# Three attention units transposed by DMA instead of TensorE, and a hand-written order of 1,080 steps laid out anew

## The chip, the cores and the metric

The kernel runs on one core of a Trainium2 chip. The metric is the device time of one execution in microseconds (us). Before the change it is 202.87 us, the median of three runs (202.74 to 204.03).

A core has five instruction queues, each of which takes its instructions strictly in order: TensorE (PE in the profile, with its weight loads as PEld), VectorE (DVE), ScalarE (ACT), GpSimd (POOL) and SyncE (SP). PE writes to PSUM, the matmul memory; the other operands lie in SBUF. Loads and stores are DMAs, issued here from SP, from POOL and at two places from ACT.

## The reference

Attention with a decay, in blocks of 64 positions, and behind it a two-layer network with a leaky rectifier. Cut to what is computed:

```python
# q, k, v: [4, 8, 768, 64]; lam: one decay for each of 8 heads
for b in range(768 // 64):
    qb, kb, vb = q[:, :, sl], k[:, :, sl], v[:, :, sl]
    intra = einsum(einsum(qb, kb) * Dmask, vb)      # within the block, masked by lam**(i-j)
    inter = einsum(qb * lam_pow, kv_state)          # from the blocks before
    out[:, :, sl] = intra + inter
    kv_state = lam_block * kv_state + einsum(kb * rev_pow, vb)
x = out.transpose(0, 2, 1, 3).reshape(3072, 512)
h = x @ w_in                                        # 512 x 2048
g = maximum(h, 0) + alpha * minimum(h, 0)
result = g @ w_out                                  # 2048 x 512, float32
```

## The kernel before

**Tiling.** The 3,072 rows are cut into six chunks `c` of 512 (two batches of 256 positions each). The attention of a chunk is four units `n` = 4c to 4c+3: two batches `bi` times two halves `hh` of the heads. Units 0 to 3 feed chunk 0, units 4 to 7 chunk 1, and so on. The network runs for a chunk when its four units are done.

**One unit.** `load` brings q and k as float32 in halves of 256 KB (quarters of a chunk's 1 MB) or whole, from SP, or from POOL where its last argument is "G". `load_v16` (line 268) brings v through POOL, cast to fp16 on the way. `cast(n, "q16", E)` and `cast(n, "k16", E)` (257) make fp16 copies `qk` on engine E: "A" is ACT, "V" DVE, "G" POOL. The copies are transposed into `qkT`, in one of two ways: `turn` (309) does four (or eight) 128 by 128 transposes on PE into a PSUM bank, and `turn_copy` (323) brings them to SBUF on E; `turned` (299) does all of it as one DMA transpose from SP. Then come `score_products` (PE), `masked` (DVE, times the decay mask), `inter` and `intra` (PE, into the accumulator), `attended` (the accumulator to SBUF on ACT or DVE), and for the running state `key_decayed`, `state_products`, `states` or `state_in` and `first_state`. `decayed` scales the transposed q. There is one PSUM buffer `s` for the scores, so `score_products` of a unit waits until `masked` of the unit before has read it. Units 0 to 8 are transposed on PE, units 9 to 23 by DMA.

**The network.** `up(c, f)` is one 512 by 128 column of h (four matmuls of 512 rows), `relu` (ACT) and `prelu` (DVE) make g from it. Chunk 0 multiplies g by `w_out` in the plain way, with `down(0, t, part)`, four matmuls each; `part` p needs block p of `w_out`, which `load_wout(p)` brings. The later chunks use sums of blocks in place of some of the products: `w_sum` forms sums of `w_out`, `in_sum` of `w_in`, `g_sum` of g and `x_sum` of x, each a run of elementwise operations on DVE or, with "G", on POOL; `second` and `last` are the products of the second layer, and `first` those of the first layer for chunks 4 and 5. `first_x`, `first_d`, `second_x` and `second_out` put the results together.

**What sets the order.** The schedule is manual. Every engine's queue holds its instructions in the order of the calls from line 799 to the end. Three things besides data hold an engine up: a free PSUM bank (four of them rotate among transposes, h, y and state products), `gate` (111), a two-byte DMA on SP that reads a piece of `w_out` and so holds SP's later loads until that block has landed, and the pair `vector_turn(i)` / `gpsimd_waits(i)` (560, 563): the first remembers the newest DVE instruction, the second makes the newest POOL instruction wait for it. There are 21 such waits before the change.

Of the kernel before, what the change touches and what calls it, by code (L numbers as in the profile page):

```python
# [11 lines left out]
def kernel(  # L12
# [503 lines left out]
    def prelu_half(c, f, bi):  # L516
        prelu_of(c, f, bi, "V")
# [341 lines left out]
    key_decayed(3)  # L859
    turn(2, (1,))  # L860
    first_state(1)
    inter(1)
    turn(3, (0,))
    turn_copy(2, (1,), "A")
    turn_copy(2, (0,), "V")
    masked(0)
    intra(1)
    score_products(2)
    decayed(2)
    turn_copy(3, (0,), "V")  # L870
    state_in(2, 0)
    first_state(0)
    masked(2)
    decayed(3)
    attended(1, "A")
    first_state(2)
    state_in(2, 1)
    turn(3, (1,))
    load(1, 0, "q", 0, "G")
    inter(0)  # L880
    load(1, 0, "k", 0, "G")
    load_v16(4)
    intra(0)
    load_win(2)
    states(2, (1,))
    slopes_turn()
    load(1, 0, "q", 1, "G")
    state_in(3, 0)
    turn_copy(3, (1,), "A")
    score_products(3)  # L890
    attended(0, "A")
    load(1, 0, "k", 1, "G")
    query_decay(2, 0)
    slopes()
    inter(2)
    intra(2)
    first_state(3)
    load(1, 1, "q", 0, "G")
    masked(3)
    state_in(1, 1)  # L900
    state_in(3, 1)
    attended(2, "A")
    states(3, (1,))
    state_in(0, 1)
    inter(3)
    states(1, (1,))
    intra(3)
    up(0, 4, 0)
    attended(3, "A")
    load(1, 1, "k", 1, "G")  # L910
    up(0, 5)
    states(0, (1,))
    relu(0, 5)
    cast(4, "q16", "G")
    up(0, 7)
    prelu(0, 5)
    up(0, 6)
    relu(0, 4, 0)
    prelu_half(0, 4, 0)
    load_wout(0)  # L920
    up(0, 3)
    key_decayed(4)
    relu(0, 7)
    up(0, 15)
    relu(0, 6)
    load_v16(5)
    prelu(0, 7)
    up(0, 13)
    relu(0, 3)
    prelu(0, 6)  # L930
    load(1, 1, "q", 1, "G")
    up(0, 14)
    relu(0, 15)
    prelu(0, 3)
    relu(0, 13)
    prelu(0, 15)
    prelu(0, 13)
    up(0, 4, 1)
    up(0, 0)
    up(0, 1)  # L940
    relu(0, 14)
    state_products(4, None, True)
    relu(0, 4, 1)
    prelu_half(0, 4, 1)
    relu(0, 0)
    prelu(0, 14)
    load_wout(1)
    relu(0, 1)
    turn(4, (0,))
    prelu(0, 0)  # L950
    prelu(0, 1)
    cast(5, "q16", "G")
    up(0, 10)
    up(0, 2)
    first_state(4)
    turn_copy(4, (0,), "V")
    turn(5, (0,))
    states(4, (1,))
    relu(0, 10)
    relu(0, 2)  # L960
    cast(4, "k16", "G")
    up(0, 11)
    cast(5, "k16", "A")
    relu(0, 11)
    decayed(4)
    prelu(0, 10)
    turn_copy(5, (0,), "V")
    up(0, 8)
    in_sum(1, 1, "G")
    turn(4, (1,))  # L970
    prelu(0, 2)
    load_wout(2)
    relu(0, 8)
    inter(4)
    cast(6, "q16", "A")
    prelu(0, 11)
    up(0, 9)
    turn_copy(4, (1,), "V")
    relu(0, 9)
    turn(5, (1,))  # L980
    load_wout(3)
    turn_copy(5, (1,), "V")
    up(0, 12)
    relu(0, 12)
    score_products(4)
    down(0, 3, 0)
    prelu(0, 9)
    prelu(0, 8)
    decayed(5)
    prelu(0, 12)  # L990
    key_decayed(5, "A")
    turn(6, (0,))
    down(0, 0, 0)
    masked(4)
    down(0, 2, 0)
    score_products(5)
    w_sum(1, 1)
    gate(2, "out")
    intra(4)
    in_sum(1, 3)  # L1000
    in_sum(1, 0, "G")
    state_products(5)
    first_state(5)
    load(1, 1, "k", 0)
    cast(7, "q16", "G")
    turn_copy(6, (0,), "V")
    w_sum(1, 2)
    key_decayed(7)
    down(0, 0, 1)
    states(5, (1,))  # L1010
    query_decay(0, 0)
    load_v16(7)
    down(0, 3, 1)
    down(0, 2, 1)
    turn(7, (0,))
    masked(5)
    down(0, 3, 2)
    attended(4, "V")
    cast(7, "k16", "G")
    turn_copy(7, (0,), "V")  # L1020
    down(0, 2, 2)
    turn(7, (1,))
    down(0, 0, 2)
    turn_copy(7, (1,), "A")
    inter(5)
    w_sum(2, 2)
    down(0, 2, 3)
    decayed(6)
    score_products(7)
    cast(6, "k16", "V")  # L1030
    intra(5)
    load(2, 0, "k", 0)
    load(2, 0, "q", None)
    query_decay(1, 0)
    state_products(7)
    first_state(7)
    down(0, 1, 0)
    w_sum(1, 3, "G")
    down(0, 3, 3)
    attended(5, "A")  # L1040
    key_decayed(6, "V")
    vector_turn(1)
    query_decay(3, 0)
    masked(7)
    w_sum(2, 3)
    down_copy(0, 2)
    decayed(7)
    w_sum(2, 1, "G")
    load_v16(6)
    down(0, 0, 3)  # L1050
    turn(6, (1,))
    states(7, (1,))
    load_v16(8)
    down_copy(0, 3)
    load(2, 1, "k", None)
    w_sum(1, 0)
    inter(7)
    load(2, 0, "k", 1)
    key_decayed(8)
    gpsimd_waits(1)  # L1060
    w_sum(2, 0, "G")
    w_sum(3, 1)
    down(0, 1, 1)
    cast(8, "k16", "A")
    load_v16(9)
    up(1, 3, 0)
    turn_copy(6, (1,), "V")
    score_products(6)
    down_copy(0, 0)
    cast(9, "q16", "A")  # L1070
    cast(8, "q16", "A")
    intra(7)
    w_sum(4, 3)
    vector_turn(2)
    state_in(6, 0)
    w_sum(3, 0, "G")
    gpsimd_waits(2)
    relu(1, 3, 0)
    turn(8, (0, 1))
    attended(7, "A")  # L1080
    first_state(6)
    down(0, 1, 2)
    masked(6)
    inter(6)
    intra(6)
    turn_copy(8, (0, 1), "V")
    prelu_half(1, 3, 0)
    state_products(8)
    score_products(8)
    w_sum(4, 1, "G")  # L1090
    gpsimd_waits(2)
    state_in(6, 1)
    key_decayed(10, "A")
    attended(6, "V")
    down(0, 1, 3)
    cast(9, "k16", "A")
    states(8, (0, 1))
    up(1, 15)
    up(1, 14)
    load(2, 1, "q", 0)  # L1100
    states(6, (1,))
    relu(1, 15)
    down_store(0, 3)
    load(3, 0, "q", None)
    down_copy(0, 1)
    load(2, 1, "q", 1)
    cast(10, "k16", "A")
    up(1, 7)
    prelu(1, 15)
    key_decayed(9)  # L1110
    relu(1, 7)
    turned(9)
    masked(8)
    up(1, 11)
    decayed(8)
    load_v16(14)
    cast(10, "q16", "G")
    relu(1, 14)
    load(3, 1, "k", 1)
    relu(1, 11)  # L1120
    prelu(1, 7)
    up(1, 6)
    relu(1, 6)
    cast(11, "k16", "A")
    inter(8)
    prelu(1, 14)
    w_sum(3, 2, "G")
    prelu(1, 11)
    up(1, 0)
    prelu(1, 6)  # L1130
    up(1, 8)
    relu(1, 0)
    prelu(1, 0)
    up(1, 13)
    score_products(9)
    relu(1, 8)
    load(3, 1, "k", 0)
    relu(1, 13)
    intra(8)
    load_v16(12)  # L1140
    prelu(1, 8)
    state_products(9)
    cast(12, "q16", "A")
    cast(11, "q16", "G")
    up(1, 12)
    up(1, 5)
    relu(1, 12)
    load_v16(10)
    masked(9)
    prelu(1, 13)  # L1150
    decayed(9)
    prelu(1, 12)
    up(1, 3, 1)
    relu(1, 5)
    attended(8, "A")
    up(1, 2)
    cast(13, "q16", "A")
    turned(10)
    g_sum(1, 1, 1, 1, "G")
    up(1, 1)  # L1160
    key_decayed(11)
    prelu(1, 5)
    load(3, 0, "k", None)
    relu(1, 3, 1)
    load_v16(13)
    relu(1, 2)
    g_sum(1, 3, 1, 1, "G")
    up(1, 4)
    states(9, (0, 1))
    w_sum(3, 3, "G")  # L1170
    relu(1, 1)
    in_sum(1, 2, "G")
    inter(9)
    prelu_half(1, 3, 1)
    prelu(1, 2)
    prelu(1, 1)
    up(1, 9)
    up(1, 10)
    relu(1, 4)
    relu(1, 9)  # L1180
    turned(11)
    down_store(0, 2)
    relu(1, 10)
    intra(9)
    prelu(1, 4)
    score_products(10)
    prelu(1, 9)
    prelu(1, 10)
    cast(13, "k16", "A")
    state_products(10)  # L1190
# [718 lines left out]
```

## Time and profile before

| | before |
|---|---|
| median of three runs | 202.87 us |
| the profiled execution, whole | 202.76 us |
| its span, first to last instruction | 201.0 us |
| granted TensorE clock, mean | 0.998 |
| DMA packets | 30.53 MB, 152 GB/s over the span |

The profile is of one execution. The 1.8 us between its time and its span lie around the program. Busy time of PE is the time in which a matmul is under way; matmuls are pipelined, so the cost of one in a run is the distance from its start to the next one's, which is shorter than its own duration. In the timeline, rows of like instructions are merged: "x8" with a start and a length, and in brackets the idle time before them and what ended it.

### The profile page before, as it was taken

How to read it: one execution, taken by the hardware profiler on the slowest of the kernel's cores; microseconds unless marked ns; L12 is line 12 of the kernel's file. 1: busy time of each engine (PE TensorE's matmuls, PEld its weight loads, DVE VectorE, ACT ScalarE, POOL GpSimd, SP SyncE). 2: the span in 40 equal slices, each digit the busy share in tenths (PEclk: the TensorE clock that was granted, in tenths of full speed). 3: DMA queues.
4: the chain of work that ended last, by engine and by line, in shares of the span. 5: the costliest groups of instructions: out<-in, count | busy, mean ns of one | idle time of the engine just before them, and what ended most of it. 6: DMA issues, size and time to landing. Idle time of an engine off the chain costs nothing. (4 is left out here: it accounts for less than half of the span.)

```text
span 201.0 us, 5883 instructions
## 1 busy us (share of the span) xinstructions
PE 193.1 (96%) x2351; PEld 129.3 (64%) x2351; DVE 169.9 (85%) x309; ACT 133.3 (66%) x296; POOL 154.1 (77%) x171
## 2 busy tenths in 40 slices
PE   7889999999999999999999999998999999999892
PEld 7766445556545688665556758775656566888792
DVE  6787998958899997999999998899999999993610
ACT  4886768229788799885688784347587886742021
POOL 8999999777999469999999989942877027559900
PEclk9999999999999999999999999999999999999999
DMA  5999999999999999999999971010310101031053
GB/s 155 265 226 225 251 255 230 200 239 281 229 193 228 298 209 214 194 185 205 201 197 220 141 164 69 3 55 0 106 52 5 54 0 52 3 104 52 19 180 117
DMA packets 59199, 30.53 MB, mean 152 GB/s; under 512 B 29652, under 2 KB 57956, under 8 KB 59172
## 3 DMA queue, kind: packets, MB, share of 16 engines
q1 hardware_dynamic: 41236, 19.87, 41.6%
q0 software_dynamic: 17776, 10.23, 33.2%
q8 instruction: 18, 0.29, 0.6%
q14 instruction: 9, 0.07, 0.1%
q10 hardware_dynamic: 160, 0.07, 0.1%
HBM read 27.27 MB, written 6.29 MB: 167 GB/s over the span
## 5 line engine op out<-in xcount | busy, mean ns | idle before, releaser
L498 PE MATMUL h_ps<-xT,w_in_sb 128*128 128x512 f16 (+1 forms) x264 | 59.4, 373 | 0.0
L655 PEld LDWEIGHTS <-g 128*128 128x128 f16 x464 | 44.6, 98 | 8.9
L526 DVE SCALAR_TENSOR_TENSOR g<-m,oma,h_ps 128x512 f16<-128x512 f32 (+1 forms) x66 | 46.0, 725 | 3.7 <-ACT m L511 2.2
L511 ACT ACTIVATE m<-h_ps 128x512 f32<-128x512 f32 (+1 forms) x66 | 36.7, 584 | 14.5 <-PE h_ps L498 13.7
L498 PEld LDWEIGHTS <-w_in_sb 128*128 128x128 f16 x264 | 24.7, 98 | 24.8
L388 DVE TENSOR_TENSOR sm<-s,dmask 128x1024 f16<-128x1024 f32 x24 | 29.2, 1217 | 2.0 <-PE s L377 1.8
L655 PE MATMUL y<-w_out_sb,g 128*128 128x256 f16 x224 | 27.1, 273 | 0.0
L341 POOL TENSOR_TENSOR qdT<-qkT,qdecay 128x512 f16<-128x512 f16 (+1 forms) x23 | 23.7, 1038 | 2.8 <-DVE qkT L249 2.0
L655 PE MATMUL b<-t,g 128*128 128x256 f16 x160 | 19.9, 273 | 0.0
L272 POOL DMA_DIRECT2D v<-in_v_dram x24 | 18.9, 789 | 0.0
L290 ACT ACTIVATE kdec<-kraw,kdecay 128x64 f16<-128x64 f32 x72 | 18.0, 341 | 0.0
L247 ACT ACTIVATE xT<-acc 128x512 f16<-128x512 f32 x21 | 12.5, 596 | 8.0 <-PE acc L422 5.4
L457 DVE SCALAR_TENSOR_TENSOR R<-R,rdecay,acc 128x128 f16<-128x128 f16 x54 | 15.5, 339 | 0.8 <-ACT xT L247 0.6
L576 POOL TENSOR_TENSOR s<-g,g 128x512 f16<-128x512 f16 x10 | 11.4, 1151 | 5.9 <-DVE g L526 5.9
L573 POOL TENSOR_TENSOR g<-g,g 128x512 f16<-128x512 f16 x12 | 14.1, 1198 | 2.3 <-DVE g L526 1.3
L534 PE MATMUL o_ps<-w_out_sb,g 128*128 128x512 f16 x64 | 15.4, 380 | 0.0
L247 ACT ACTIVATE o_sb<-y 128x512 f32<-128x512 f32 (+2 forms) x12 | 6.3, 524 | 10.5 <-PE y L697 5.4
L573 POOL TENSOR_TENSOR g<-s,g 128x512 f16<-128x512 f16 x5 | 5.9, 1174 | 9.5 <-DVE g L573 9.5
L292 POOL TENSOR_TENSOR kdec<-kraw,kdecay 128x512 f16<-128x512 f32 x12 | 12.7, 1061 | 0.5 <-DMA kraw<-in_k_dram 0.5
L573 POOL TENSOR_TENSOR g<-g 128x512 f16<-128x512 f16 x10 | 11.4, 1154 | 1.1 <-DVE g L526 0.7
L576 POOL TENSOR_TENSOR w_in_sb<-g,g 128x512 f16<-128x512 f16 x3 | 3.9, 1285 | 9.0 <-DVE g L526 9.0
L377 PE MATMUL s<-qkT 64*64 64x128 f16 x384 | 9.8, 220 | 0.9 <-DVE sm L388 0.9
(131 smaller groups left out, 381.7 us busy)
## 6 DMA issues: line engine op xcount, KB each, us to landing
out_dram<-o_sb SPq DMA_DIRECT2D x23, 256.0 KB, 2.4
kraw<-in_k_dram SPq DMA_DIRECT2D x7, 512.0 KB, 6.0
qraw<-in_q_dram SPq DMA_DIRECT2D x6, 512.0 KB, 5.6
v<-in_v_dram POOLq DMA_DIRECT2D x24, 128.0 KB, 6.0
w_in_sb<-in_moe_w_in_dram POOLq DMA_DIRECT2D x4, 512.0 KB, 8.6
w_out_sb<-in_moe_w_out_dram POOLq DMA_DIRECT2D x4, 512.0 KB, 9.4
qraw<-in_q_dram POOLq DMA_DIRECT2D x6, 256.0 KB, 7.3
qraw<-in_q_dram SPq DMA_DIRECT2D x6, 256.0 KB, 6.6
```

The source lines that it names most:

```text
L247: nc.scalar.activation(out, in_, AF.Copy)
L272: nc.gpsimd.dma_start(out=v16.rearrange("p h e d -> p h (e d)"), in_=v[2 * (c % 2) + bi, ds(4 * hh, 4), ds((c // 2) * W, W), :].rearrange( ...
L290: nc.scalar.activation(kdec[:, e, h], kr[:, e, h], AF.Copy, scale=kdecay[:, x, e : e + 1])
L341: engine(eng).tensor_tensor(out=qdT[:, :, :, p], in0=(t["qps"] if eng == "P" else t["qkT"][:, 0])[:, :, :, p], in1=qdecay[:, hh, :, :, p], ...
L388: nc.vector.tensor_tensor(out=t["sm"].rearrange("p a h x j -> p (a h) x j"), in0=t["s"].rearrange("p a h x j -> p (a h) x j"), in1=mask_of ...
L457: nc.vector.scalar_tensor_tensor(out=R[b, hh, m + 1][:, hp], in0=R[b, hh, m][:, hp], scalar=rdecay[:, 2 * hh + hp : 2 * hh + hp + 1], in1= ...
L498: nc.tensor.matmul(h[:, 0:n] if bi is None else h[:, 0:n].rearrange("p (e j) -> p e j", e=2), lhsT=w_in_sb[:, gi, ts(f, 128)], rhs=x.rearr ...
L511: nc.scalar.activation(m[:, 0:n], HP[c, f, bi][:, 0:n], AF.Relu, scale=-1.0)
L526: engine(eng).scalar_tensor_tensor(out=g, in0=m, scalar=oma[:, f : f + 1], in1=h, op0=ALU.mult, op1=ALU.add)
L534: nc.tensor.matmul(O[c, t], lhsT=g_of(c, f)[:, t // 2, t % 2, :], rhs=w_out_sb[:, f, :], start=(f == 0), stop=(f == NF - 1),)
L573: engine(eng).tensor_tensor(out=out, in0=a, in1=b, op=ALU.subtract)
L655: nc.tensor.matmul(Y[c, k][:, ds(b * HALF, HALF)], lhsT=left(c, i, f, b), rhs=right(i, f), start=(f == 0 and b == 0 and i in (1, 5)), stop ...
```

## The change

The first 60 calls of the order stay. Behind them:

- Units 6, 7 and 8 are transposed with `turned` (SP) in place of `turn` and `turn_copy`: 24 transposes on PE and five copies (four on DVE, one on ACT) go, three DMA transposes come.
- All calls behind the first 60 are in a new order. Among others, unit 7 comes before unit 6, `load_win(2)` and two halves of unit 7's data are issued before the data of units 4 and 5, `load_wout(0)` to `load_wout(3)` come earlier in the order, and more of the `down` products of chunk 0 stand ahead of `score_products(5)`.
- 79 calls change engine, with the same arithmetic: casts, `turn_copy`, `w_sum`, `g_sum`, `in_sum`, `x_sum`, `attended`, `decayed`. Of the last chunks (4 and 5), ten `g_sum` go from POOL to DVE and five the other way.
- The waits of POOL for DVE are 29 in place of 21.

The lines that matter most here, from the diff (it has 1,819 lines):

```diff
@@ -857,1022 +857,1028 @@
     decay_mask(0)
     score_products(0)
     key_decayed(3)
+    first_state(1)
     turn(2, (1,))
-    first_state(1)
+    state_in(1, 1)
+    first_state(0)
+    masked(0)
     inter(1)
+    intra(1)
     turn(3, (0,))
+    load_win(2)
+    turn_copy(2, (0,), "V")
     turn_copy(2, (1,), "A")
...
+    load(1, 1, "q", 1, "G")
+    turn(3, (1,))
+    decayed(2, "V")
+    attended(1, "A")
     score_products(2)
...
-    load(1, 0, "q", 0, "G")
-    inter(0)
-    load(1, 0, "k", 0, "G")
-    load_v16(4)
     intra(0)
-    load_win(2)
...
-    load(1, 0, "q", 1, "G")
...
+    state_in(3, 1)
+    load(1, 0, "k", 0, "G")
+    inter(2)
+    masked(3)
+    load(1, 1, "k", 1, "G")
+    first_state(3)
+    load(1, 0, "q", 0, "G")
...
+    load_v16(4)
...
+    state_in(2, 1)
     load(1, 0, "k", 1, "G")
-    query_decay(2, 0)
+    load(1, 0, "q", 1, "G")
     slopes()
...
     up(0, 4, 0)
+    load_wout(0)
     attended(3, "A")
-    load(1, 1, "k", 1, "G")
+    load_wout(1)
+    relu(0, 4, 0)
+    in_sum(1, 2, "G")
+    up(0, 4, 1)
+    states(3, (1,))
+    up(0, 6)
+    up(0, 3)
...
     key_decayed(4)
+    up(0, 0)
+    relu(0, 14)
+    load(1, 1, "q", 0, "G")
     relu(0, 7)
-    up(0, 15)
...
+    cast(5, "q16", "G")
+    cast(7, "q16", "V")
     prelu(0, 7)
     up(0, 13)
...
+    load_wout(2)
+    relu(0, 2)
+    cast(7, "k16", "G")
+    cast(4, "q16", "A")
+    state_products(4, None, True)
+    prelu(0, 10)
     relu(0, 13)
-    prelu(0, 15)
+    key_decayed(7)
+    load_wout(3)
+    gate(2, "out")
+    prelu(0, 2)
+    w_sum(1, 0, "G")
+    up(0, 8)
+    turn(5, (0,))
+    load(1, 1, "k", 0)
+    first_state(4)
+    prelu(0, 0)
+    load(2, 0, "k", 0)
     prelu(0, 13)
-    up(0, 4, 1)
-    up(0, 0)
-    up(0, 1)
-    relu(0, 14)
-    state_products(4, None, True)
...
+    cast(4, "k16", "V")
+    vector_turn(1)
+    prelu(0, 9)
     turn(4, (0,))
-    prelu(0, 0)
-    prelu(0, 1)
-    cast(5, "q16", "G")
-    up(0, 10)
-    up(0, 2)
-    first_state(4)
+    in_sum(1, 0, "G")
+    gpsimd_waits(1)
     turn_copy(4, (0,), "V")
-    turn(5, (0,))
+    relu(0, 11)
+    load_v16(5)
+    down(0, 3, 0)
+    prelu(0, 11)
+    turn(4, (1,))
+    decayed(4)
+    down(0, 2, 0)
+    up(0, 12)
+    load_v16(6)
+    relu(0, 12)
+    turn_copy(4, (1,), "A")
+    down(0, 3, 1)
+    query_decay(2, 0)
+    down(0, 2, 1)
     states(4, (1,))
-    relu(0, 10)
-    relu(0, 2)
-    cast(4, "k16", "G")
...
+    in_sum(1, 3)
+    vector_turn(2)
+    prelu(0, 12)
+    score_products(4)
+    turn(5, (1,))
+    down(0, 0, 0)
+    cast(6, "q16", "G")
     inter(4)
-    cast(6, "q16", "A")
-    prelu(0, 11)
...
     decayed(5)
-    prelu(0, 12)
     key_decayed(5, "A")
-    turn(6, (0,))
-    down(0, 0, 0)
+    w_sum(1, 1, "G")
+    gpsimd_waits(2)
+    down(0, 2, 2)
+    w_sum(2, 1, "G")
+    gpsimd_waits(2)
+    down(0, 3, 2)
+    turn_copy(5, (1,), "A")
+    w_sum(4, 1)
     masked(4)
-    down(0, 2, 0)
+    down(0, 3, 3)
+    turned(7)
+    w_sum(1, 2)
+    down(0, 2, 3)
     score_products(5)
-    w_sum(1, 1)
-    gate(2, "out")
+    w_sum(2, 0)
+    vector_turn(3)
+    load_v16(7)
+    down_copy(0, 3)
...
     intra(4)
-    in_sum(1, 3)
-    in_sum(1, 0, "G")
     state_products(5)
+    cast(6, "k16", "A")
     first_state(5)
...
-    cast(7, "q16", "G")
-    turn_copy(6, (0,), "V")
-    w_sum(1, 2)
-    key_decayed(7)
...
+    cast(8, "k16", "G")
+    load_v16(8)
+    query_decay(1, 0)
+    load(2, 0, "q", None)
...
+    key_decayed(6, "V")
+    w_sum(1, 3)
+    vector_turn(4)
     states(5, (1,))
     query_decay(0, 0)
-    load_v16(7)
-    down(0, 3, 1)
-    down(0, 2, 1)
-    turn(7, (0,))
     masked(5)
-    down(0, 3, 2)
-    attended(4, "V")
-    cast(7, "k16", "G")
-    turn_copy(7, (0,), "V")
-    down(0, 2, 2)
-    turn(7, (1,))
+    down(0, 1, 0)
+    down(0, 1, 1)
+    load_v16(9)
+    decayed(7, "V")
+    vector_turn(5)
+    down(0, 1, 2)
+    turned(6)
...
-    turn(8, (0, 1))
...
+    turned(8)
...
+    g_sum(5, 2, 1, 1)
+    vector_turn(18)
     second(4, 5, 1)
-    second_store(3, 7)
-    prelu(5, 15)
-    g_sum(4, 2, 0, 1)
-    g_sum(5, 1, 1, 1, "G")
-    second(5, 2, 0)
-    second(5, 2, 1)
+    second(5, 5, 1)
+    g_sum(5, 2, 0, 1, "G")
...
```

## What I predicted

> **What bounds the kernel now.** I read the page first: busy time, then the slices.
>
> ```profile
> span 201.0 us, 5883 instructions
> ...
> PE 193.1 (96%) x2351; PEld 129.3 (64%) x2351; DVE 169.9 (85%) x309; ACT 133.3 (66%) x296; POOL 154.1 (77%) x171
> ...
> PE   7889999999999999999999999998999999999892
> ...
> DVE  6787998958899997999999998899999999993610
> ...
> PEclk9999999999999999999999999999999999999999
> DMA  5999999999999999999999971010310101031053
> ```
>
> PE is busy for nine tenths or more of nearly every slice from the fourth on, at full clock: the kernel is PE's stream with a start and a tail. The DMA row matters too: its engines are full to slice 23, about 115 us. How little PE waits stands in the view of waits, PE alone; only these two lie behind the start:
>
> ```profile
> PE b L780 <- DVE e L576: 0.6, 1, 0.6
> PE y L697 <- POOL g L573: 0.6, 1, 0.6
> ```
>
> So a saving counts only if it shortens PE's stream or one of these waits, and any new wait of PE is paid in full. I add up against this execution, 202.76 us with its 1.8 us around the span; that is 0.11 under the median of 202.87.
>
> **Term 1, the transposes.** Five groups go, for units 6, 7 and 8: 24 transposes. PE's timeline has the cost of a group as the distance to the next row:
>
> ```profile
> 27.18 1.89 PE L498 MATMUL h_ps<-xT,w_in_sb 128*128 128x512 f16 x8
> 28.90 0.39 PE L316 MATMUL tp<-ident,qk 128*128 128x128 f16 x4
> ...
> 34.45 0.39 PE L316 MATMUL tp<-ident,qk 128*128 128x128 f16 x4
> 34.68 1.89 PE L534 MATMUL o_ps<-w_out_sb,g 128*128 128x512 f16 x8
> ...
> 36.75 0.39 PE L402 MATMUL acc<-sm,v 64*64 64x128 f16 x16
> 36.97 0.29 PE L422 MATMUL acc<-v,kdec 64*64 64x64 f16 x16
> ...
> 49.68 0.62 PE L316 MATMUL tp<-ident,qk 128*128 128x128 f16 x8
> 50.13 1.03 PE L534 MATMUL o_ps<-w_out_sb,g 128*128 128x512 f16 x4
> ```
>
> Four cost 34.68 - 34.45 = 0.23, eight 0.45: in all four fours and the eight, 4 x 0.23 + 0.45 = 1.37 us off the stream. The first two rows give the price of an `up` or a `down`: 1.72 / 8 x 4 = 0.86; the rows at 36.75 and 36.97 that of one group of attention products, 0.22. The mean length of one transpose, from the groups by form, is no price, as lengths overlap:
>
> ```profile
> L316 PE MATMUL tp<-ident,qk 128*128 128x128 f16 x72 | 6.5, 220 | 0.6 <-DVE qk L249 0.6
> ```
>
> [...]
>
> The copies that go (four on DVE, one on ACT) are hidden: PE waited for neither engine there. The three DMA transposes come on SP:
>
> ```profile
> qkT<-qk SPq DMA_TRANSPOSE x15, 4.7
> ...
> DMA to landing us min/median/max: 3.0/4.7/8.3
> ```
>
> `turned(7)` has its casts early and stands behind the gate on `w_out` block 2 and two loads (about 40 us); PE comes to `score_products(7)` at about 48 (below), so it is hidden even at 8.3. `turned(6)` and `turned(8)` have 7 to 9 us; price zero, and up to 2 us at the longest time. Behind them on SP stand only loads for chunk 2.
>
> **Term 2, a wait that comes in.** POOL's queue decides here. `cast(5, "q16", "G")` needs the half `load(1, 0, "q", 1)`. Before, two halves, one v and a block of `w_in` were issued ahead of it (behind the third `w_in` block); now it is the last of eight: `load_win(2)`, six halves, one v. Eight of the same sizes followed that block before, too, in another order; here are the block and the eighth (timeline, then the DMA issues of two short windows):
>
> ```profile
> 10.81 0.83 POOL L98 DMA_DIRECT2D w_in_sb<-in_moe_w_in_dram  x1
> ...
> 21.72 0.75 POOL L89 DMA_DIRECT2D kraw<-in_k_dram  x1 [0.36 <-DMA w_in_sb<-in_moe_w_in_dram]
> ```
>
> ```profile
> w_in_sb<-in_moe_w_in_dram POOLq DMA_DIRECT2D x1, 512.0 KB, 10.6
> ...
> kraw<-in_k_dram POOLq DMA_DIRECT2D x1, 256.0 KB, 8.3
> ```
>
> The block landed at 10.8 + 10.6 = 21.4, the eighth at 21.7 + 8.3 = 30.0, so eight such transfers take 8.6 us with the DMA engines full. The prefix is the same, the eight are the same sizes: I expect `load(1, 0, "q", 1)` at 30.0, however early it is issued. Before, the cast ran here:
>
> ```profile
> 27.43 0.61 POOL L251 CAST qk<-qraw 128x512 f16<-128x512 f32 x1 [0.18 <-DMA qraw<-in_q_dram]
> 27.99 0.61 POOL L251 CAST qk<-kraw 128x512 f16<-128x512 f32 x1
> 28.60 0.67 POOL L341 TENSOR_TENSOR qdT<-qkT,qdecay 128x256 f16<-128x256 f16 x1
> 29.23 1.15 POOL L576 TENSOR_TENSOR s<-w_in_sb 128x512 f16<-128x512 f16 x1
> 30.33 1.53 POOL L104 DMA_DIRECT2D w_out_sb<-in_moe_w_out_dram  x2
> ...
> 34.49 1.04 POOL L292 TENSOR_TENSOR kdec<-kraw,kdecay 128x512 f16<-128x512 f32 x1
> 35.48 0.79 POOL L272 DMA_DIRECT2D v<-in_v_dram  x1
> ...
> 38.37 1.15 POOL L573 TENSOR_TENSOR t<-w_out_sb 128x512 f16<-128x512 f16 x1
> ```
>
> Queued behind it on POOL, by these rows: the cast 0.61, two `w_out` issues 1.53, casts of 7 and 6 1.22, `key_decayed(7)` 1.04, two v issues 1.58, `decayed` 4 and 5 1.34, and four sums (`w_sum(1,0)`, `in_sum(1,0)`, `w_sum(1,1)`, `w_sum(2,1)`) 4.60: 11.9 us, so `w_sum(2,1)` ends at 30.1 + 11.9 = 42.0. DVE's `w_sum(4,1)` reads its result, and `masked(4)` is the next on DVE. Durations of both, by form:
>
> ```profile
> L388 DVE TENSOR_TENSOR sm<-s,dmask 128x1024 f16<-128x1024 f32 x24 | 29.2, 1217 | 2.0 <-PE s L377 1.8 <-ACT R L449 0.3
> ...
> L573 DVE TENSOR_TENSOR t<-w_out_sb 128x512 f16<-128x512 f16 x3 | 1.3, 425 | 0.0
> ```
>
> `masked(4)` ends at 42.0 + 0.1 + 0.43 + 1.22 = 43.75, and `score_products(5)` needs the one `s` buffer. When would PE be there? Its first `up` starts
>
> ```profile
> 17.94 4.28 PE L498 MATMUL h_ps<-xT,w_in_sb 128*128 128x256 f16 x21
> ```
>
> at 17.94 before; now about 0.3 later, as `decayed(2)` and two `states` stand in DVE's way, but the second half of column 4 then fills the pause in which PE waited for `attended(3)`; both halves are done by 19.25 either way, and I count the start at zero (bounds -0.3 and +0.5). From there 15 `up` and 9 `down` at 0.86, four transpose groups and four attention groups at 0.22 come to 20.6 + 1.8 = 22.4: PE is there at 41.7. New wait: 43.75 - 41.7 = 2.05 us, in two parts, 0.8 at `turn(5, (0,))` (needs the cast) and the rest at the scores. Bounds: none, if the cast runs at 28 or earlier; 3.2, if the eight transfers take a tenth longer and the four sums the 1.23 of POOL's last run (below).
>
> **Term 3, v of unit 7.** `load_v16(7)` is issued behind `w_sum(2,1)`, at 42. Before, the two v loads issued beside SP's loads landed like this:
>
> ```profile
> v<-in_v_dram POOLq DMA_DIRECT2D x2, 128.0 KB, 6.8
> ```
>
> That gives 48.9. PE reaches `state_products(7)` after three `down` and nine attention groups, at 43.75 + 2.6 + 2.0 = 48.4: 0.4 us of wait; 0 to 2, at the 8.3 of the half above.
>
> **Term 4, the end.** Ten `g_sum` of chunks 4 and 5 leave POOL for DVE, five go the other way. Before, POOL's last run set the wait at `last`:
>
> ```profile
> 184.53 6.15 POOL L573 TENSOR_TENSOR g<-g,g 128x512 f16<-128x512 f16 x5
> ...
> 188.32 1.05 PE L697 MATMUL y<-w_out_sb,g 128*128 128x256 f16 x8 [0.62 <-POOL g L573]
> ```
>
> DVE, with time to spare there, does a sum in 0.43 against 6.15 / 5 = 1.23, so that wait goes: -0.6. The other one (0.6 at `first`, for DVE) I halve, -0.3: `x_sum` keep their length, but DVE has less to do before them. Next behind both is PE itself.
>
> **The eight more waits of POOL for DVE.** Those in the chain of term 2, (1) and the two (2), wait for DVE steps that stand ahead of `prelu(0, 12)`, over by 36, when POOL's sums behind the late cast are not yet begun: zero. Waits 18 to 20 hold the last three `g_sum` of POOL behind DVE's; nothing but these sums is queued there, and PE needs them for `last` and `second(4, 3)`, four and more products of 0.9 us later: zero, up to one sum's 1.2 if DVE is late. The others hold casts, `decayed` and sums a whole unit ahead of their use; I take zero, with one DVE sum (0.43) as the bound on both sides.
>
> All other moved calls are price zero, covered by a stream without waits; DVE is the thin cover between 60 and 130 us (85% over the whole span, nine tenths and more there), so 0 to +1 lies in it.
>
> **Sum.** 202.76 - 1.37 + 2.05 + 0.4 - 0.6 - 0.3 = 202.94, about 203.0: no change that a measurement tells. I take 1%, 2.0 us, as what it can tell from none.
>
> **Rivals.**
>
> *The wait does not come.* If the cast of unit 5 runs at 28 or before, the chain ends before PE needs it, and v of unit 7 is in time: 202.76 - 1.37 - 0.9 = 200.5. For it: PE waits for no load before, so the order of loads was workable. Against it: the eight transfers' 8.6 us. Chance 0.28.
>
> *The loads grow late, and it is slower.* SP now has two loads, a transpose and a 512 KB load under way while POOL asks for v of units 6, 7 and 8. If v of unit 7 takes not 6.8 but the 10.6 of the `w_in` row, PE waits until 52.6, 4.2 us in place of 0.4: 202.94 + 3.8 = 206.7. It decides (over 1% slower, 204.9) from a landing time of 8.8. For it: full DMA engines; against it: no v or transpose row over 8.3. [...] Chance 0.17.
>
> *A transpose costs PE its whole length.* If each held PE for its 0.22, 24 would give 5.3 instead of 1.37: 202.94 - 3.9 = 199.0. The distances of the rows speak against it. Chance 0.03.
>
> **How the numbers follow.** Forecast 0.52 (its own range 202.0 to 204.4). Faster by over 1% is below 200.85: two thirds of the first rival and the third, 0.22. Slower by over 1%: the second rival and the forecast's edge, 0.18. Within 1%: 0.60. The range 200.3 to 205.5 leaves the upper half of the slow case and the third rival out.
>
> **What would show it.** Right: the cast of unit 5's q on POOL at 30; on DVE an idle stretch of some 5 us up to 42, ended by POOL `t` L573; PE waiting about 1 us for DVE `sm` at L377; no POOL wait of PE at L697; PE's busy sum lower by less than 2. Wrong: that cast at 28, PE full from 20 to 54, chunk 1's second `up` before 52.5 (then the first rival); a PE wait for a DMA of v or qkT over 1.5 us (the second). The forecast fails if eight transfers take clearly less than 8.6 us, or if DVE between 60 and 130 makes PE wait.

## The result, and the profile after

The changed kernel takes 204.98 us, the median of 18 runs (203.91 to 206.54); the kernel before, timed with it, 203.10 us (202.67 to 204.27). The ratio is 1.0085, with a 95% interval of 1.0064 to 1.0107: slower by 0.85%, inside the 1% that I counted as no change. It lies inside the range of 200.3 to 205.5, near its upper end, but above the forecast's own range of 202.0 to 204.4; in place of the 0.1 to 0.2 us that the sum added, 1.9 came. The profiled execution took 205.40 us. Two profiles of the experiments below are of disturbed executions: that of `e11_all` is the longest of its ten (207.28 us), and that of `e12_robust` (1103 us, PE busy for 1097.4 us in place of 194.8) is used for nothing.

The page of the changed kernel, busy time and slices:

```profile
span 203.6 us, 5831 instructions
...
PE 194.8 (96%) x2327; PEld 128.6 (63%) x2327; DVE 173.2 (85%) x308; ACT 132.1 (65%) x294; POOL 148.3 (73%) x169
...
PE   7887999999999999999999999999999999999992
...
PEclk9998899999999999999999999999999999999999
```

24 matmuls are gone (2,351 to 2,327), and yet PE's busy sum grew from 193.1 to 194.8. PEclk is below 9 in two slices near 20 us; before, it was 9 all through. The waits of PE, which before had two lines behind the start:

```profile
PE s L377 <- DVE sm L388: 1.7, 2, 1.2
...
PE y L655 <- DVE g L526: 0.4, 1, 0.4
PE acc L402 <- DVE sm L388: 0.3, 1, 0.3
...
PE b L780 <- DVE d L576: 0.2, 1, 0.2
PE b L655 <- POOL g L573: 0.2, 1, 0.2
```

The wait at L697 is gone, and that at L780 for `e` fell from 0.6 to 0.3, both as foretold. Nearly all that came is for DVE.

Where did the time go? For each matmul I take the distance from its start to the next one's start, and the median of that distance for its kind over the profiles. The medians, added up, are the stream; what a distance has above its median is loss, added up by stretch of the profile:

| us | before | after | after - before |
|---|---|---|---|
| the stream | 180.5 | 179.2 | -1.3 |
| loss, 0 to 10 | 1.62 | 1.51 | -0.1 |
| loss, 10 to 30 | 3.67 | 6.41 | +2.7 |
| loss, 30 to 60 | 2.11 | 2.83 | +0.7 |
| loss, 60 to 130 | 5.97 | 6.31 | +0.3 |
| loss, 130 to 200 | 2.07 | 2.47 | +0.4 |
| start of the last matmul | 197.03 | 199.83 | +2.8 |

The transposes brought what I had put down for them. The loss grew by 4.1, nearly two thirds of it ahead of 30 us, where I had counted zero. (With other ways of telling the kinds apart the stream differs by 1.2 to 1.4, and the 0.3 between 60 and 130 us moves to the stretch before it; the rest stays.)

**The start.** Timelines of DVE, POOL and PE in the changed kernel:

```profile
14.00 1.65 DVE L341 TENSOR_TENSOR qdT<-qkT,qdecay 128x256 f16<-128x256 f16 x1
15.57 1.21 DVE L388 TENSOR_TENSOR sm<-s,dmask 128x1024 f16<-128x1024 f32 x1
...
13.76 1.13 POOL L292 TENSOR_TENSOR kdec<-kraw,kdecay 128x512 f16<-128x512 f32 x1
14.75 0.83 POOL L98 DMA_DIRECT2D w_in_sb<-in_moe_w_in_dram  x1
...
16.84 0.42 PE L377 MATMUL s<-qkT 64*64 64x128 f16 x16 [1.24 <-DVE sm L388]
...
19.61 11.72 PE L498 MATMUL h_ps<-xT,w_in_sb 128*128 128x256 f16 x52
```

`decayed(2, "V")` takes 1.65 us; the same shape takes 0.42 elsewhere (below). It began 0.24 us behind POOL's `key_decayed(3)` and ended at 15.65, just as POOL's DMA issue ended (14.75 + 0.83 = 15.58). So `masked(2)` is late, and PE waits 1.24 us at the scores of unit 3. Then windows of one microsecond on PE (length, busy, granted clock, DMA):

```profile
16.00:17.00 1.00, 0.16 (x12) 1.00 1.25 209
...
18.00:19.00 1.00, 0.94 (x24) 0.82 1.24 214
19.00:20.00 1.00, 1.00 (x19) 0.50 1.24 200
...
21.00:22.00 1.00, 1.00 (x5) 0.50 1.27 215
22.00:23.00 1.00, 1.00 (x6) 0.97 1.14 337
```

Some three microseconds after the pause began, the clock is halved for about 3.4 us (0.18 + 3 x 0.50 + 0.03 = 1.7 us of PE's time). This does not come every time: in six of the 18 runs the mean clock is 0.99, with a median span of 203.6; in the other twelve it is 1.00, with 202.7. The profiled execution, and with it the table above, is one of the six; at full clock the kernel is slower than the one before all the same.

**Term 2's place.** POOL, DVE and PE again:

```profile
29.86 0.60 POOL L251 CAST qk<-qraw 128x512 f16<-128x512 f32 x1 [1.08 <-DMA qraw<-in_q_dram]
...
40.87 1.15 POOL L573 TENSOR_TENSOR t<-w_out_sb,t 128x512 f16<-128x512 f16 x1
...
42.06 0.43 DVE L573 TENSOR_TENSOR t<-w_out_sb,t 128x512 f16<-128x512 f16 x1 [2.68 <-POOL t L573]
42.40 1.22 DVE L388 TENSOR_TENSOR sm<-s,dmask 128x1024 f16<-128x1024 f32 x1
...
44.73 0.42 PE L377 MATMUL s<-qkT 64*64 64x128 f16 x16
```

The chain came to the tenth: the cast at 29.9 (30 foretold), the last sum of POOL over at 42.02 (42.0), `masked(4)` over at 43.62 (43.75). But PE comes to the scores of unit 5 only at 44.73, not at 41.7, and waits for nothing there. It was late already.

**Late.** DVE and POOL between 143 and 179 us, and PE's wait:

```profile
145.31 1.73 DVE L526 SCALAR_TENSOR_TENSOR g<-m,oma,d 128x512 f16<-128x512 f32 x1
...
143.11 2.27 POOL L573 TENSOR_TENSOR x<-xT,x 128x512 f16<-128x512 f16 x2
145.34 1.15 POOL L573 TENSOR_TENSOR g<-s,g 128x512 f16<-128x512 f16 x1
...
148.55 0.59 PE L780 MATMUL b<-x,w_in_sb 128*128 128x512 f16 x2 [0.20 <-DVE d L576]
...
176.65 1.43 DVE L526 SCALAR_TENSOR_TENSOR g<-m,oma,d 128x512 f16<-128x512 f32 x1
...
174.15 3.38 POOL L573 TENSOR_TENSOR g<-g 128x512 f16<-128x512 f16 x3
```

Two `prelu` that read only SBUF (`m` and `d`) take 1.73 and 1.43 in place of 0.74, each beside POOL sums. What the end had won at the other waits was lost again here.

### The profile page after: what moved, and what is told of

It reads as the page before. It is cut to its first block, busy times and chain, and to the rows that moved or that the text cites. A ratio compares the mean times of both kernels' runs of the same rounds, so it can differ in the third digit from the quotient of the medians.

```text
span 203.6 us, 5831 instructions
## 1 busy us (share of the span) xinstructions
PE 194.8 (96%) x2327; PEld 128.6 (63%) x2327; DVE 173.2 (85%) x308; ACT 132.1 (65%) x294; POOL 148.3 (73%) x169
## 4 chain that ended last, share of the span: by engine, by line
PE 77%; DVE 15%; ACT 3%; issue 2%; POOL 1%; ACTq 0%; DVEq 0%; POOLq 0%
PE h_ps L498 26%; PE y L655 12%; PE b L655 12%; PE o_ps L534 5%; DVE g L526 5%; PE b L780 3%; PE s L377 3%; PE acc L402 3%; DVE sm L388 3%; PE a L780 3%; PE unread L145 2%; PE e L780 2%; PE acc L361 2%; ACT m L511 1%; PE acc L422 1%
## 5 line engine op out<-in xcount | busy, mean ns | idle before, releaser
L498 PE MATMUL h_ps<-xT,w_in_sb 128*128 128x512 f16 (+1 forms) x264 | 60.8, 379 | 0.0
L511 ACT ACTIVATE m<-h_ps 128x512 f32<-128x512 f32 (+1 forms) x66 | 37.7, 582 | 20.6 <-PE h_ps L498 20.3
L498 PEld LDWEIGHTS <-w_in_sb 128*128 128x128 f16 x264 | 25.1, 100 | 25.8 <-issue 0.7
L341 POOL TENSOR_TENSOR qdT<-qkT,qdecay 128x512 f16<-128x512 f16 (+1 forms) x21 | 22.1, 1053 | 0.9 <-DVE w_out_sb L573 0.8
L247 ACT ACTIVATE xT<-acc 128x512 f16<-128x512 f32 x23 | 13.7, 594 | 12.3 <-PE acc L402 6.8
L573 POOL TENSOR_TENSOR g<-g,g 128x512 f16<-128x512 f16 x11 | 12.9, 1173 | 8.2 <-PE y L655 5.7
L573 POOL TENSOR_TENSOR g<-s,g 128x512 f16<-128x512 f16 x7 | 8.4, 1211 | 9.7 <-DVE g L573 9.0
L780 PEld LDWEIGHTS <-w_in_sb 128*128 128x128 f16 x64 | 6.3, 98 | 6.8 <-issue 1.0
L402 PE MATMUL acc<-sm,v 64*64 64x128 f16 x384 | 10.0, 223 | 0.4 <-DVE sm L388 0.3
L576 POOL TENSOR_TENSOR w_in_sb<-g,g 128x512 f16<-128x512 f16 x3 | 3.4, 1156 | 9.2 <-DVE g L526 9.2
```

Source lines behind the costliest of these rows:

```text
L247: nc.scalar.activation(out, in_, AF.Copy)
L341: engine(eng).tensor_tensor(out=qdT[:, :, :, p], in0=(t["qps"] if eng == "P" else t["qkT"][:, 0])[:, :, :, p], in1=qdecay[:, hh, :, :, p], ...
L498: nc.tensor.matmul(h[:, 0:n] if bi is None else h[:, 0:n].rearrange("p (e j) -> p e j", e=2), lhsT=w_in_sb[:, gi, ts(f, 128)], rhs=x.rearr ...
L511: nc.scalar.activation(m[:, 0:n], HP[c, f, bi][:, 0:n], AF.Relu, scale=-1.0)
L573: engine(eng).tensor_tensor(out=out, in0=a, in1=b, op=ALU.subtract)
L780: nc.tensor.matmul(t, lhsT=w, rhs=x, start=(g == 0 and i in (1, 5)), stop=(g == 1), skip_group_check=True)
```

## The experiments

Each short diff is against the changed kernel, unless another is named; ratios are to the kernel before, timed on the same chip, with their 95% interval.

**E1: `decayed(2)` from PSUM.**

```diff
-    decayed(2, "V")
+    decayed(2, "P")
```

> DVE's decayed(2) reads q from PSUM, as before the change, in place of SBUF. Theory A (the late start and the late chain of POOL overlap: whichever is later decides): decayed(2) takes about 0.43 us in place of 1.65, masked(2) starts a microsecond earlier, PE does not fall idle at score_products(3) for 1.2 us, the granted clock stays near 1.0 through 16 to 23 us, and the first up starts near 18 in place of 19.6. But w_sum(2,1) on POOL still ends near 42 and masked(4) near 43.7, so PE then waits about 2 us for DVE's sm at the scores of unit 5, and the whole gains only 0.3 to 1.0 us: about 204.2. Theory B (the start's loss is carried to the end in full, the chain of POOL does not bind): no such wait at the scores of unit 5, gain about 2.6 us: about 202.4.

The expectation calls this "as before the change", which is not so: before, `decayed(2)` ran on POOL, from SBUF (its default engine; the two L341 on POOL from 14.78 us), and the change moved it to DVE. The only L341 operation on DVE before was `decayed(1, "P")`, 0.43 us from PSUM.

Measured 204.49 us (204.02 to 205.04), 1.0051 (1.0027 to 1.0074), an interval that overlaps that of the changed kernel. The operation is short again:

```profile
14.62 0.41 DVE L341 TENSOR_TENSOR qdT<-tp,qdecay 128x256 f16<-128x256 f16 x1
```

The clock stayed at 1.00 (all ten runs have 0.997 or more), the first `up` started at 18.98. But the median span is 202.7, that of the changed kernel's runs at full clock: what is gained is the clock, and the earlier start is lost again before the end. PE comes to the scores of unit 5 at 43.52, with no wait, so neither theory is right: the chain does not bind, and the start is not carried through.

**E2 and E3: `masked(4)` ahead of `w_sum(4, 1)`**, with and without E1's edit.

```diff
-    w_sum(4, 1)
     masked(4)
+    w_sum(4, 1)
```

> As the first kernel, and masked(4) stands ahead of w_sum(4,1) on DVE, so that the mask of unit 4 no longer waits for POOL's sum. Theory A: the wait at the scores of unit 5 goes with it, masked(4) ends before 41.5, and the time falls by a further 1 to 2 us: about 202.5. Theory B: same as the first kernel within 0.3 us, as that wait did not bind.

> Only masked(4) ahead of w_sum(4,1); the start stays as in the changed kernel. Theory A: PE comes to the scores of unit 5 at 44.7, when masked(4) had long ended either way, so nothing is gained: 204.9 within 0.4. Theory B: the same, nothing. If it gains over 0.5 us, the late chain cost time elsewhere on DVE or PE, and both theories miss it.

E2: 204.65 us, 1.0058 (1.0034 to 1.0083), the same as E1; the mask was over at 40.15 and PE still came at 43.55. E3: 206.12 us of four runs, 1.0108 (1.0058 to 1.0158), no gain; three of the four have a mean clock of 0.988. The late chain of POOL cost nothing by itself in any kernel.

**E4: keep PE busy in its pause.**

```diff
     state_in(3, 0)
+    tick(20)
     score_products(3)
```

> Twenty spare 128x128 products on PE between state_in(3,0) and score_products(3), which keep it busy through its 1.2 us of waiting for DVE; they write a bank nobody reads. If the idle time is what lowers the granted clock, the clock stays above 0.9 from 18 to 23 us in place of 0.5, though decayed(2) still takes 1.65 us. Theory A: the first ups then run 1.7 us faster, PE waits instead at the scores of unit 5 (about 0.7 to 1 us), and the time falls by 0.7 to 1.0: about 204.1. Theory B: by 1.7: 203.3. If the clock falls all the same, the idle time is not its cause, and the time is that of the changed kernel plus what the products take.

Measured 205.35 us, 1.0088 (1.0056 to 1.0120): no gain, though eight of the nine runs have a mean clock of 1.00. The profile is of the ninth, the longest (207.15 us, 0.992). The twenty products filled the pause, and the clock stayed at 1.00 up to 21 us; then

```profile
21.17 5.09 PE L498 MATMUL h_ps<-xT,w_in_sb 128*128 128x256 f16 x19 [1.84 <-DVE R L457]
```

PE paused behind `states` instead, most likely because the spare products had taken one of the four banks, and the clock fell to 0.50 from 22 to 25 us, again after a pause. Filling the pause did not help here, with DVE as late as before: the eight runs at full clock have a median span of 203.6 us, against 202.7 of the changed kernel's.

**E8: the same operation, POOL kept away.** E1 moved the operand, so it could not tell a slow source from a busy neighbour.

```diff
     decayed(2, "V")
+    vector_turn(30)
+    key_decayed(3)
+    gpsimd_waits(30)
+    load_win(2)
+    load(1, 1, "q", 1, "G")
```

(the three POOL calls leave their old places).

> decayed(2) on DVE reads SBUF as in the changed kernel, but POOL's key_decayed(3), load_win(2) and the load behind it are put behind it by a wait, so that POOL does nothing meanwhile. Theory contention (the operation waits until POOL's instruction is over): decayed(2) takes 0.43 us in place of 1.65, PE's wait at score_products(3) shrinks to under 0.5 us, no half clock, and the time is that of the kernel with decayed(2) from PSUM, or up to 0.7 us more, as POOL's work starts later: 204.5 to 205.2. Theory source (SBUF in place of PSUM makes it slow by itself): still 1.65 us, and the time of the changed kernel or more: 205.0 to 206.5.

DVE and POOL in this kernel:

```profile
14.88 0.42 DVE L341 TENSOR_TENSOR qdT<-qkT,qdecay 128x256 f16<-128x256 f16 x1
...
15.38 1.05 POOL L292 TENSOR_TENSOR kdec<-kraw,kdecay 128x512 f16<-128x512 f32 x1 [1.02 <-DVE qdT L341]
```

0.42 us from the same SBUF operands: it is the neighbour. Measured 204.83 us (204.28 to 205.30), 1.0080 (1.0043 to 1.0117), as the theory of contention said; no run has a mean clock under 0.997. By what means POOL holds DVE up is not shown. The 1.65 lasted 0.76 us beyond the end of `key_decayed` (14.89), through a DMA issue (see the last section).

The kept traces (all but E12's) say the same of all DVE operations of this sort, that is of its casts, sums, `decayed`, `key_decayed` and the `prelu` of `d`, whose operands lie in SBUF. Of those that overlapped arithmetic of POOL, 231 of the 241 that began after POOL took longer than alone, by more than 0.05 us, and none of the 89 that began first (in the traces of the two kernels alone 36 of 39, and none of 14). The `prelu` of a whole column from PSUM (0.73 to 0.75) and `masked` (1.21 to 1.23) kept their length beside POOL in every case.

**E5: the start of the kernel before.** Calls 61 to 109 as before the change (the loads of unit 7 kept early), and `masked(4)` ahead of `w_sum(4, 1)`; `decayed(2)` is back on POOL. The edit is some 50 moved lines, of which these matter:

```diff
-    turn(3, (1,))
-    decayed(2, "V")
...
+    decayed(2)
...
+    load(1, 1, "q", 1, "G")
+    load(1, 0, "k", 1, "G")
...
     up(0, 4, 0)
+    load(1, 1, "k", 1, "G")
```

> Calls 61 to 109 in the order and on the engines of the kernel before (with the two halves of unit 7's q and k still early, so that the later casts find them), then the rest of the changed order, with masked(4) ahead of w_sum(4,1). Theory A (what is left of the loss after the first experiments lies ahead of the first up, and is carried to the end): the first up starts at about 17.95 in place of 18.6 to 19.6, no half clock, load(1,0,q,1) is the fifth of the eight transfers, and the time is about 1 us under that of the kernel with decayed(2) from PSUM: 203.4. Theory C (DVE's own operations on SBUF, slowed beside POOL between 25 and 50 us, hold PE up, so that an earlier start is only waited off there): PE's waits for DVE g between 27 and 36 us grow from 0.9 to about 1.9 us and the time stays at 204.3.

Measured 205.22 us, 1.0112 (1.0068 to 1.0157): theory C in what held PE up, though 0.9 us over its 204.3. The first `up` starts at 17.82, 1.2 us ahead of E1's, and then:

```profile
27.99 0.77 DVE L249 CAST qk<-qraw 128x512 f16<-128x512 f32 x1 [1.65 <-DMA qraw<-in_q_dram]
...
29.47 1.02 PE L498 MATMUL h_ps<-xT,w_in_sb 128*128 128x512 f16 x4 [1.28 <-DVE g L526]
```

DVE stands 1.65 us at `cast(7, "q16", "V")`, whose data land at 27.97; the `prelu` queued behind it are late, and PE waits for a bank. In E1 the same place cost 0.37, the cast taking 0.96 beside POOL, and another 0.5 came at 34 us, from the other cast that the change gave to DVE:

```profile
32.49 1.35 DVE L249 CAST qk<-kraw 128x512 f16<-128x512 f32 x1
...
31.82 1.06 POOL L292 TENSOR_TENSOR kdec<-kraw,kdecay 128x512 f16<-128x512 f32 x1
32.82 0.79 POOL L104 DMA_DIRECT2D w_out_sb<-in_moe_w_out_dram  x1
```

**E9: the late meetings undone** (with E1's edit).

```diff
-    g_sum(3, 2, 1, 0, "G")
...
     vector_turn(14)
+    g_sum(3, 2, 1, 0, "G")
+    gpsimd_waits(14)
...
-    g_sum(3, 2, 0, 1, "G")
+    g_sum(3, 2, 0, 1)
...
     prelu(5, 14)
+    vector_turn(30)
...
     g_sum(5, 3, 0, 0, "G")
+    gpsimd_waits(30)
```

> decayed(2) from PSUM, and two late meetings of DVE and POOL undone: the POOL sum g_sum(3,2,1,0) waits for prelu(5,8), g_sum(3,2,0,1) goes to DVE, and the POOL sum g_sum(5,3,0,0) waits for prelu(5,14). Theory contention: the two prelu take about 0.75 to 0.85 us in place of 1.74 and 1.45, PE's waits near 147.5, 148.6 and 178.7 us (0.36 + 0.32 + 0.53 in lost distance) go, and the time falls by 0.9 to 1.2 us against the kernel with decayed(2) alone: 203.4. Rival: PE is held up there by its own chain of data (the sums themselves are late), the prelu get shorter but the waits stay or turn up behind: 204.3.

Measured 203.81 us (203.52 to 204.81), 1.0023 (0.9995 to 1.0050): 0.28% under E1, 0.6 us, though the intervals overlap. The loss of 140 to 150 us fell from 1.14 to 0.54. Near 178 us it stayed, and the trace (of the longest of the ten, 204.81 us) says why:

```profile
175.97 0.74 DVE L526 SCALAR_TENSOR_TENSOR g<-m,oma,d 128x512 f16<-128x512 f32 x1
...
177.15 1.19 DVE L573 TENSOR_TENSOR g<-s,g 128x512 f16<-128x512 f16 x1
...
176.79 1.27 POOL L573 TENSOR_TENSOR g<-g 128x512 f16<-128x512 f16 x1 [1.04 <-DVE g L526]
...
179.06 1.16 PE L655 MATMUL y<-w_out_sb,g 128*128 128x256 f16 x9 [0.44 <-DVE g L526]
```

The `prelu` is short again (0.74), but POOL's sum, now later, meets the next DVE sum (1.19 in place of 0.43), and the `prelu` behind that is late. Here the wait moved the meeting and did not end it.

**E10: start, casts and late meetings.** E5 and E9, but `load_win(2)` second of the eight transfers and unit 7's q the last, the second late wait behind `prelu(4, 15)`, and against E5:

```diff
     prelu(0, 3)
+    cast(4, "k16", "V")
...
-    cast(7, "q16", "V")
...
-    cast(4, "k16", "V")
...
     states(4, (1,))
+    cast(7, "q16", "V")
```

> The start of the kernel before as in the run with that start, load_win(2) as the second of the eight transfers, and DVE's two casts out of the way of the prelu of chunk 0: cast(7,q16) goes behind states(4,(1,)), so that DVE waits for no load, and cast(4,k16) to the stretch near 24.6 us in which POOL waits; the two late meetings undone, the second now by a wait for prelu(4,15). Theory C (PE was held up between 26 and 36 us by DVE behind its own casts): PE's waits for DVE g between 25 and 36 us fall from 1.9 us to under 0.4, PE reaches the scores of unit 5 near 42.3 in place of 44.1, and the late gain of 0.5 us near 178 comes too: 202.0. Rival (POOL's chain to w_sum(2,1), cast(5,q16) in front): cast(5) still runs at 28 to 29 and turn(5,(0,)) then waits for it; PE reaches the scores of unit 5 at 43 or later, and the time is 203 or more.

Measured 202.72 us, ratio 0.9997 (0.9956 to 1.0038). The profiled execution (span 200.6) is as theory C says: no wait for DVE `g` between 25 and 36 us, and the scores of unit 5 start at 42.20. The late gain did not come: PE still waits 0.29 us for `g` near 179 us. And the runs form two groups, six at 202.2 to 202.8 and four at 204.6 to 205.8. Here is the moved cast in the profiled execution, one of the six, and POOL's next instruction:

```profile
24.73 0.42 DVE L249 CAST qk<-kraw 128x512 f16<-128x512 f32 x1
...
24.84 0.75 POOL L104 DMA_DIRECT2D w_out_sb<-in_moe_w_out_dram  x1 [1.58 <-DMA w_in_sb<-in_moe_w_in_dram]
```

DVE comes first by 0.1 us, at the end of a stretch in which POOL waits for a load.

**E11: two more waits of PE.** Against E10:

```diff
+    masked(5)
     states(5, (1,))
     query_decay(0, 0)
-    masked(5)
...
     gate(1, "out")
+    load(4, 1, "q", None)
...
-    load(4, 1, "q", None)
...
+    cast(18, "q16", "G")
     load_v16(22)
     load_v16(18)
...
-    cast(18, "q16", "G")
```

> As the kernel before it in this call, and masked(5) ahead of states(5) on DVE, so that intra(5) does not wait 0.5 us for it near 47 us, and cast(18,q16) with its load earlier, so that the DMA transpose of unit 18 lands ahead of its scores near 108 us (0.5 to 0.9 us of lost distance). If every wait of PE is paid in full: 1.0 us less than that kernel, 201.0. If DVE is simply short of time up to 130 us, so that a wait taken away comes back later: no difference over 0.3.

Measured 203.38 us, 1.0018 (0.9980 to 1.0057): no gain; by the medians it is 0.7 us slower than E10, which neither text foretold, with intervals that overlap. Its runs too form groups, seven at 202.8 to 204.0 and three at 205.4 to 207.3. The wait near 47 us went, but PE now waited 1.9 us for a DMA transpose up to 103.5 us, and my guess, which no run tests, is the load that I put ahead of it on SP (92.24 us, the transposes from 95.29). What the trace of its longest execution shows is the other side of E10's cast:

```profile
25.77 2.59 DVE L249 CAST qk<-kraw 128x512 f16<-128x512 f32 x1
...
25.14 0.75 POOL L104 DMA_DIRECT2D w_out_sb<-in_moe_w_out_dram  x1 [1.56 <-DMA w_in_sb<-in_moe_w_in_dram]
25.91 1.17 POOL L576 TENSOR_TENSOR s<-w_in_sb 128x512 f16<-128x512 f16 x1
27.02 1.05 POOL L292 TENSOR_TENSOR kdec<-kraw,kdecay 128x512 f16<-128x512 f32 x1
```

DVE comes 0.6 us after POOL, and stands until 28.36 behind three POOL instructions in a row: 2.59 us in place of 0.42, and PE waits 1.8 us behind it. That this is what parts the two groups of E10 and E11 rests on these two traces, and on E12.

**E12: the cast off the edge.** Against E10, with `masked(5)` as in E11:

```diff
     prelu(0, 5)
+    cast(4, "k16", "V")
...
-    cast(4, "k16", "V")
...
-    vector_turn(30)
...
-    g_sum(5, 3, 0, 0, "G")
-    gpsimd_waits(30)
...
     g_sum(5, 3, 1, 1)
+    g_sum(5, 3, 0, 0)
```

> As the kernel with the start, casts and late meetings, with three more changes: cast(4,k16) one place earlier on DVE (behind prelu(0,5), in the middle of the stretch of 1.6 us in which POOL waits for a load, in place of its edge), masked(5) ahead of states(5), and g_sum(5,3,0,0) on DVE behind g_sum(5,3,1,1) in place of POOL. Theory contention: the runs near 204.7 us go (the cast no longer meets POOL), 0.4 us of PE's wait near 46 us and 0.45 near 178.7 go too, and the time is 201.8. Rival: the two groups of times come from elsewhere (the loads, the start); a third of the runs stays near 204.5 and the median at 202.5.

Seven of the eight runs lie at 201.15 to 202.61 us, median 202.00, and the eighth is that of 1103 us; over the seven the ratio is 0.9914 (0.9881 to 0.9948). The group at 204.7 is gone, and this version beats both kernels: by the ratios 0.9% under the one before, 1.7% under the changed one. The time foretold, 201.8, is 0.2 off. Where the cast now lies is seen in E13, which has this order:

```profile
23.12 0.42 DVE L249 CAST qk<-kraw 128x512 f16<-128x512 f32 x1
...
24.83 0.75 POOL L104 DMA_DIRECT2D w_out_sb<-in_moe_w_out_dram  x1 [1.57 <-DMA w_in_sb<-in_moe_w_in_dram]
```

It is over 1.3 us ahead of the end of POOL's idle stretch, and E13's ten runs form one group as well (203.77 to 204.78).

**E13 and E6: what is a transpose worth?** E13 is E12 with 48 spare products; E6 (with E1's edit) puts units 6 to 8 back on PE.

```diff
     up(1, 14)
+    tick(16)
```

```diff
-    turned(8)
...
     up(1, 6)
+    turn(8, (0, 1))
+    turn_copy(8, (0, 1), "A")
```

> As the other kernel of this call, with 48 spare 128x128 products on PE, sixteen behind each of up(1,14), up(1,8) and up(1,13), into banks nobody reads; the size of a transpose, twice as many as the change removes, and without copies. If PE's stream is the bound there and a transpose is worth its distance of 0.057 us: 2.7 us more than the other kernel. If PE has slack there that they fill: less than 1 us. If each costs its own length of 0.22: 10 us.

> decayed(2) from PSUM as in the first experiment, and units 6, 7 and 8 transposed on PE again, eight transposes at a time with the copy on ACT, in place of the three DMA transposes. If the transposes were worth the 1.37 us of their distances, and the DMA transposes cost nothing: 1.4 us over the kernel with decayed(2) alone: 205.9. If the DMA transposes delay other transfers or the scores: less than 0.7 us more, or even less than before (205.2 or lower). If a transpose costs PE its whole length: 5 us more, 209.

E13: 204.23 us (203.77 to 204.78), 1.0047 (1.0021 to 1.0074), 1.33% over E12: 2.7 us, with an uncertainty of 0.9 from the two intervals (2.2 by the medians). In the trace the first group of sixteen costs 53.85 - 52.96 = 0.89:

```profile
52.96 1.06 PE L145 MATMUL unread<-ident 128*128 128x128 f16 x16
53.85 4.48 PE L498 MATMUL h_ps<-xT,w_in_sb 128*128 128x512 f16 x20
```

that is 0.056 each, and PE has no slack there. Of the waits of PE that the view lists for E13, only one lies behind 20 us:

```profile
PE b L780 <- DVE e L576: 0.3, 1, 0.3
```

E6: 207.75 us, 1.0245 (1.0200 to 1.0290), 1.9% over E1, some 3.9 us (3.3 by the medians), where 1.4 was expected. Its groups of eight cost 0.45, as before; the rest is loss that came with the edit, of which this is one piece:

```profile
59.06 0.61 PE L316 MATMUL tp<-ident,qk 128*128 128x128 f16 x8
59.51 1.03 PE L498 MATMUL h_ps<-xT,w_in_sb 128*128 128x512 f16 x4
60.84 1.02 PE L498 MATMUL h_ps<-xT,w_in_sb 128*128 128x512 f16 x4 [0.31 <-ACT qkT L247]
```

An `up` waits for the bank that ACT's copy still holds. Where the other 2 us lie was not traced to single waits. So E6 does not price the removal; it says only that transposes put back in this way cost more than their distances.

## Why the prediction was right, and where its steps failed

**Base: right.** PE's stream bounds the kernel: E13's 48 added products, 0.056 us each, are paid in full (2.7 us).

**Term 1: right in size.** -1.37 foretold, -1.3 in the stream. The third rival, the whole length of each transpose, is refuted for products of this size: E13 would have been 10 us slower. The DMA transposes cost nothing in the changed kernel, where no wait of PE for `qkT` is listed. That is no law: in E1, E2, E8 and E9 one such wait (0.3 to 0.7) appears near 110 us, at unit 18, which was transposed by DMA before the change too.

**Term 2: the chain right, the price not.** Each time of POOL's chain came within 0.15 us. The step that failed is "I count the start at zero": I named the cause, that `decayed(2)` and the `states` stand in DVE's way, and gave it 0.3 us, without a row for `decayed(2)` on DVE. The nearest row, 0.43, is of an operation that reads PSUM; with both operands in SBUF beside POOL it took 1.65. From this came a pause of PE, at times a half clock, and a first `up` at 19.61 in place of 18.2. The wait of 2.05 at the scores of unit 5 did not come, because PE was later than that: two losses in one place, of which only the larger counts. So the two errors hid each other in part, the kernel stayed within 1% by luck, and the sum was still 2 us short. That the start alone is not the answer is shown by E1, E2 and E5: with it mended, DVE's casts beside POOL (0.96 and 1.35, priced among "all other moved calls zero") held PE up instead.

**Term 3: not seen.** v of unit 7 landed at 48.07, 0.8 ahead of the forecast, and PE did not wait for it; it lost 0.5 there for `masked(5)`, which stands behind `states(5)` on DVE. E11's trace, with the order turned, has no such wait at that place.

**Term 4: half right.** The wait at `last` went and that at `first` was halved, as priced, but "next behind both is PE itself" failed: next behind were two `prelu` held up by POOL's sums. -0.9 became +0.4 in the stretch behind 130 us. E9 took back 0.6 of it there, and among the waits listed for E13 only the 0.3 at L780 remains.

**DVE as a thin cover**, 0 to +1, was the right warning in the wrong stretch: 60 to 130 us lost 0.3 at most; the loss lay at 10 to 60 and behind 140.

**The signs.** The cast at 30 and the missing wait at L697 came as named. DVE's idle stretch up to 42 was 2.7 us and not some 5, the wait for `sm` at the scores of unit 5 did not come, and PE's busy sum rose by 1.7 where it was to fall: the signs told that the time was made up otherwise than in the sum.

Still open: why the kernel before, too, has times near 202.7 and near 204.0. It has meetings of DVE and POOL as well; which of them differs between its runs was not tried.

## What to carry to other kernels

When an elementwise operation is moved to DVE, price it by a row with the same memories for its operands, and look at what POOL does at that very time: a cast that costs 0.42 us alone took 2.59 in E11, through three POOL instructions. If DVE feeds the bound, put such an operation into a stretch in which POOL waits anyway, in the middle of it (0.42 in E13), or make POOL wait, and then look whom POOL meets next. A saving on the bounding engine counts in full only if its feeders have room: here 1.3 us were saved and 4.1 lost, and the same saving, with the start of the kernel before and a few operations of DVE and POOL placed otherwise, gave the version that beats both.

## What the runs showed of the hardware that I had not expected

In the profiled execution a pause of 1.24 us of PE was followed by half the granted clock (0.50), from three microseconds after its start and for 3.4 us. A third of the runs have the low mean clock that goes with it, 0.988 to 0.990 (six of 18; in E3, with the same start, three of four have 0.988). With that pause gone (E1, E2, E8) all 25 runs have 0.997 or more. But the length of a pause does not decide alone: with E5's pause of 1.28 us near 28 us the mean clock of its four runs is 0.998 or more, and E11's trace has two pauses of over 1.8 us, up to 29.07 and up to 103.52 us, with a mean clock of 0.997, and the `up` behind them take 0.86 to 0.89 us each, against the 0.86 of full clock. What else decides is not shown. The kernel before, whose pauses behind the first microsecond are of 0.65 and less, has a mean clock of 0.996 or more in each run whose clock is on record.

Whether POOL's DMA issues hold DVE up as its arithmetic does is open. The operation of 1.65 us ended 0.07 after an issue (15.58), not after the `key_decayed` ahead of it (14.89), and E1's cast of 1.35 ended 0.23 after one (33.61). But E11's cast of 2.59 us ended 0.29 after POOL's last arithmetic (28.07), in the middle of the issue that followed (28.01 to 28.80), and of the 107 DVE operations of the sort counted under E8 that met nothing of POOL but issues, 101 kept their length (13 of 14 in the traces of the two kernels). POOL itself stood 1.0 to 1.8 us at some issues and at its cast for loads in flight (1.01 at 21.73, 1.80 at 24.28, 1.08 at 29.86 in the changed kernel).
